# First factor of a 3008-point transform: 32x32 instead of 64x64 TensorE tiles for batches 2 to 7

## The chip, the core and the metric

The kernel runs on one core of a Trainium2 chip. The metric is the device time of one execution in microseconds (us); the median of the runs counts. The engines are called as in the profile: PE is TensorE (matmuls; PEld is its weight load), DVE is VectorE, ACT is ScalarE, POOL is GpSimd and SP is SyncE, which here issues almost all DMAs.

## The reference

Two layers, one behind the other, all in fp32. The first mixes along the sequence with a filter in the frequency domain, the second is a feed-forward layer with ELU.

```python
def _attn_ref(x, filt_r, filt_i):            # x: 8 x 3008 x 256
    X = np.fft.rfft(x, axis=1)
    Y = X * (filt_r + 1j * filt_i)[None, :, :]
    return np.fft.irfft(Y, n=x.shape[1], axis=1).astype(np.float32)

def _moe_ref(x, w_in, w_out):                # x: 24064 x 256, w_in: 256 x 2048
    h = x @ w_in
    g = np.where(h > 0.0, h, np.exp(np.minimum(h, 0.0)) - 1.0)
    return g @ w_out
```

## The kernel before

The 3008 points are taken as 47 x 64. The forward transform has two factors: a 64-point one for each of the 47 residues n1 (the "first factor", with its twiddles), and a 47-point one (the "second factor"); the filter product and the two factors of the inverse follow, and then the feed-forward layer. The residues n1 = i and n1 = 47 - i are worked on together, so 24 pairs i stand for the 47 residues. They are loaded in 6 chunks of 4 pairs (`XC` = 4, `NXC` = 6).

The feed-forward layer is the bulk of the work. It runs in 192 steps, which the code calls quads: 8 batches of 6 blocks, each block with 4 quarters of the 2048 hidden columns. A step has 7 products "up" (`up_steps`, lines 568 to 648, written to the tiles phs, pha and phd by line 583) and the 7 products "down" of the step before it (`down_steps`, lines 653 to 689, written to po by line 665); 7 are enough for a 2x2 blocked product of 8. Each product is two matmul instructions of 128x128 weights and 256 columns (224 in a batch's first block), and each fp32 matmul instruction stands in the trace as two records. ACT and DVE do the ELU and the sums of the seven products.

The transform of batch b is woven into the feed-forward steps of batch b - 1. Nothing is scheduled at run time: the order of every engine is the order of the Python calls. The loop at the end of the kernel goes through the steps and emits the up and down products alternately; the table `plan` says which other pieces go where in a step: place 2 and 3 among the first products, place 0 in the middle, place 1 at the end, behind the DVE and ACT work that the step itself leaves (`up_tail`, `down_tail`). A step in which `opens` holds starts with a down product, to give the banks time. Let t be the first step of batch b - 1. For batches 2 to 7, what matters here is planned so:

- `x_load` (line 202) fetches a chunk of x and its table `ta` of cosines and sines.
- `x_unit` (line 220; DVE lines 223 and 224) forms for a chunk the sum and the difference of points n2 and n2 + 32 (tiles sd and xc). Place 0 of steps t, t + 3 and t + 4, for two chunks each.
- `a_unit` (line 230) is the first factor of two chunks: place 1 of the same steps, so three times a batch. They are called its first, second and third unit below; there are 21 in all, 18 of them for batches 2 to 7.
- `z_write` (line 305; DMA line 311), behind it at place 1, stores the result of the two chunks to DRAM (z); `z_read` (line 313; DMA line 317) brings it back, rearranged, for the second factor. The reads of the first two groups are issued at step t + 4, behind the third unit's writes; then come loads of x for the next batch.
- `b_unit` (line 378) is the second factor, from step t + 6 on, in tiles of 24x32 (sixteen tiles at once, line 388); `bi_unit` (line 450) is the corresponding one of the inverse, also in sixteen tiles (line 460). Both are planned four times a batch.
- `n_unit` (line 522; matmuls in line 535, 64x64 tiles) is the last factor of the inverse. It comes at place 0 of steps t + 1, t + 5, t + 8 and others; it takes two PSUM banks.

One `a_unit` has 16 matmul instructions of 64x64 tiles and 256 columns. A tile's 64 rows hold the points of i (32 rows) and of 47 - i (32 rows), and the 64 columns of its table hold cosines and sines with both signs, so that one matmul does the 64-point factor and joins i with 47 - i at once. Four tiles of the array work side by side. Four ACT copies (line 241) then move the four PSUM banks to two tiles t1 in SBUF.

Four PSUM banks (the list `banks`) serve all pieces but po. `bank()` takes the one that stands first in the list, and each piece appends its banks in the order in which they will be free. In a step, phs holds one bank from the first up product to the sixth, pha one for the second, and phd one from the fifth up product to the last; what a piece at place 1 takes was held by these. [...]

The batches differ at the start: batch 0 has a path of its own (`a_first`), and in the steps in which batch 1 is transformed, DVE and ACT still prepare feed-forward weights (`w_split`, `w_float`, `w_join`, `w_sums`).

Of the kernel before, what the change touches and what calls it, by code (L numbers as in the profile page):

```python
# [11 lines left out]
FP32 = mybir.dt.float32  # L12
U32 = mybir.dt.uint32
AXT = mybir.ActivationFunctionType
# [12 lines left out]
P = 128  # L27
# [14 lines left out]
def _make_tables():  # L42

    n2, k2 = np.arange(N2), np.arange(K2)
    ta, tn = np.zeros((P, H, P)), np.zeros((P, H, P))
    for i in range(H):
        for h in range(2):
            if h and i == 0:
                continue  # L60
            n1 = N1 - i if h else i
            th = 2 * np.pi * (((N1 * n2[:, None] + n1) * k2[None]) % N) / N
            c, s = np.cos(th), -np.sin(th)
            c[:, 0], s[:, 0] = 1.0, 1.0 - 2.0 * (n2 % 2)
            sign = -1.0 if h else 1.0
            r = slice(h * 64, h * 64 + 64)
            for p, v in enumerate((c, sign * s, s, sign * c)):
                ta[r, i, p * 32:p * 32 + 32] = v
                tn[p * 32:p * 32 + 32, i, r] = v.T
    tf = np.ascontiguousarray(ta.reshape(P, H, 4, K2).transpose(0, 1, 3, 2)).reshape(P, H, P)  # L70
    tb = ta.reshape(2, 2, 32, NXC, 2, 2, 4, 16, 2)[:, 0].transpose(3, 0, 1, 2, 4, 7, 5, 6)
    ta = np.ascontiguousarray(tb).reshape(P, H // 2, P)
    i = np.arange(H)[:, None]
    gb, gr, gi = (np.zeros((P, 2, 64)) for _ in range(3))
    q = np.arange(N1)[None]
    th = 2 * np.pi * ((i * np.where(q < 24, q, 70 - q)) % N1) / N1
    c, s = np.cos(th), np.sin(th)
    sign = np.where(q < 24, 1.0, -1.0)
    gb[0:24, 0, :N1], gb[24:48, 0, :N1] = c, s
    gb[64:88, 0, :N1], gb[88:112, 0, :N1] = c * sign, -s * sign  # L80
    for o in (0, 64):
        gr[o:o + N1, 0, 0:24], gr[o:o + N1, 0, 24:48] = 2 / N * c.T, 2 / N * s.T
        gi[o:o + N1, 0, 0:24], gi[o:o + N1, 0, 24:48] = 2 / N * (c * sign).T, -2 / N * (s * sign).T
    k1 = np.arange(24)[None]
    t0 = 2 * np.pi * ((i * k1) % N1) / N1
    t3 = 2 * np.pi * ((i * (32 + 64 * k1)) % N) / N
    c0, s0, c3, s3 = np.cos(t0), np.sin(t0), np.cos(t3), np.sin(t3)
    gb[0:24, 1, 0:24], gb[24:48, 1, 24:48] = c0, c3
    gb[64:88, 1, 24:48], gb[88:112, 1, 0:24] = -s3, -s0

    m0, m3 = np.full((24, 1), 2 / N), np.full((24, 1), 2 / N)
    m0[0] = m3[23] = 1 / N
    s0[:, 0] = s3[:, 23] = 0.0
    gr[0:24, 1, 0:24], gr[24:48, 1, 24:48] = m0 * c0.T, m3 * c3.T
    gi[0:24, 1, 24:48], gi[24:48, 1, 0:24] = -m0 * s0.T, -m3 * s3.T

    fb, bb = np.zeros((P, 2, 32)), np.zeros((P, 2, 4, 32))
    for p in range(4):  # L100
        r = slice(32 * p, 32 * p + 24)
        fb[r, 0, :24] = (-1.0 if p == 3 else 1.0) * gb[24 * (p % 2):24 * (p % 2) + 24, 0, 0:24]
        q = (0, 24, 64, 88)[p]
        k = 24 if p in (1, 2) else 0
        fb[r, 1, :24] = gb[q:q + 24, 1, k:k + 24]
    for o in range(0, P, 32):
        for p, (t, c) in enumerate(((gr, 0), (gr, 24), (gi, 0), (gi, 24))):
            bb[o:o + 24, 0, p, :24] = t[0:24, 0, c:c + 24]

    bb[0:24, 1, 0, :24], bb[0:24, 1, 1, :24] = gr[0:24, 1, 0:24], gr[24:48, 1, 24:48]  # L110
    bb[0:24, 1, 2, :24], bb[0:24, 1, 3, :24] = gi[24:48, 1, 0:24], gi[0:24, 1, 24:48]
    pairs = np.concatenate([fb.reshape(P, 64), bb.reshape(P, 2 * P)], 1)
    lie = np.concatenate([2 * np.arange(24), 2 * np.arange(24) + 1])
    gb[:, :, lie] = gb[:, :, :48].copy()
    for t in (gr, gi):
        for o in (0, 64):
            t[o + lie] = t[o:o + 48].copy()
    gf = np.zeros_like(gb)
    for o in (0, 64):
        gf[o:o + 48] = gb[o:o + 48].reshape(2, H, 2, 64).swapaxes(0, 1).reshape(48, 2, 64)  # L120
    tw = np.ascontiguousarray(tn[:, 0:8].reshape(4, K2, 8, 2, 2, 32).transpose(1, 0, 2, 4, 3, 5)).reshape(P, 8, P)
    tn = tn.reshape(4, K2 // 2, 2, H, 2, 2, 32)[..., 0, :] * np.array([1.0, -2.0])[:, None, None, None]
    tn = np.ascontiguousarray(tn.transpose(2, 1, 0, 3, 4, 5)).reshape(P, H, 64)
    once = np.stack([np.eye(P), gf.reshape(P, P)], 1)
    return [t.astype(np.float32) for t in (ta, tn, np.stack([gb, gr, gi], 1), tf, once, pairs, tw)]


def order(m):
# [5 lines left out]
def kernel(  # L134
# [8 lines left out]
):  # L143
    nc = tc.nc

    ta_d, tn_d, gs_d, tf_d, once_d, pairs_d, tw_d = [
        nc.inline_tensor(t, name=n + "_t").ap()
        for t, n in zip(_make_tables(), ("ta", "tn", "gs", "tf", "once", "pairs", "tw"))
    ]

    def pool(name, bufs, **kw):
# [44 lines left out]
    def bank(name, shape=(P, 2, D)):  # L196
        i = banks.pop(0)
        return i, psM.tile(list(shape), FP32, tag="m%d" % i, name=name)

    def x_load(b, c, queue=nc.sync, place=None):

        t, w = place or (xp.tile([P, 2, 2, D], FP32, tag="xc", name="xc"), tap.tile([P, 2, P], FP32, tag="ta", name="ta"))
        xs[b, c], tas[b, c] = t, w
        queue.dma_start(w, ta_d[:, 2 * c:2 * c + 2, :])
        for h in range(2):
            i = XC * c + 2 * h
            r = slice(64 * h, 64 * h + 32)
            nc.sync.dma_start(t[r].rearrange("p k u d -> p k (u d)"),  # L210
                              raw(x, b * N + i, [[N1 * D, 32], [32 * N1 * D, 2], [1, 2 * D]]))
            r = slice(64 * h + 32, 64 * h + 64)
            for u in range(2):
                if i + u == 0:
                    nc.gpsimd.memset(t[r, :, 0, :], 0.0)
                else:
                    nc.sync.dma_start(t[r, :, u, :],
                                      raw(x, b * N + N1 - i - u, [[N1 * D, 32], [32 * N1 * D, 2], [1, D]]))
# [8 lines left out]

    def a_unit(b, c):  # L230
        ps = [[bank("psa") for _ in range(2)] for _ in range(2)]
        for j in range(2):
            xt, w, sm = xs.pop((b, c + j)), tas.pop((b, c + j)), sds.pop((b, c + j))
            for u in range(2):
                for o, src in ((0, sm), (64, xt[:, 1])):
                    for (_, p), r in zip(ps[j], HALVES):
                        nc.tensor.matmul(p[o:o + 64, u, :], w[r, u, o:o + 64], src[r, u, :], start=True, stop=True)  # L237
        for j in range(2):
            t = t1s[b, c + j] = t1p.tile([P, XC, D], FP32, tag="t1", name="t1")
            for h, (i, p) in enumerate(ps[j]):  # L240
                nc.scalar.activation(out=t[:, 2 * h:2 * h + 2, :], in_=p, func=AXT.Copy)
                banks.append(i)
# [61 lines left out]

    def z_write(b, c):
        if c == 0:
            zs[b] = zp.tile([H, 4 * K2 + 1, D], FP32, tag="z", name="z")
        t = t1s.pop((b, c))
        z = zs[b][XC * c:XC * c + XC, 0:4 * K2, :].rearrange("i (q r) d -> r q i d", r=2)
        for r in range(2):  # L310
            nc.sync.dma_start(z[r], t[HALVES[r]])

    def z_read(b, g):
        t = t2[:, g % 2]
        for p in range(4):
            k = p * K2 + 4 * g
            nc.sync.dma_start(t[32 * p:32 * p + 24].rearrange("i u d -> i (u d)"),
                              zs[b][:, k:k + 4, :].rearrange("i u d -> i (u d)"))

    def f_read_first(g, t):  # L320
        for a, r in enumerate((LO, HI)):
# [517 lines left out]
    with tc.manual_schedule():  # L839
# [153 lines left out]
        for b in range(B):  # L993
            t = (b - 1) * PER
            if b > 0:
                for c, s in enumerate((2, 2, 3, 3, 4, 4) if b == 1 else (0, 0, 3, 3, 4, 4)):
                    at(t + s, 0, x_unit, b, c)
                    if c % 2 == 0:
                        opens.add(t + s + 1)
                        at(t + s, 1, a_unit, b, c)  # L1000
                    if c % 2:
                        for k in (c - 1, c):
                            at(t + s, 1, z_write, b, k)
                        if c == NXC - 1:
                            for k in range(2):
                                at(t + s, 1, z_read, b, k)
                        for k in (c - 1, c):
                            nb, nxt = (b, k + XBUFS) if k + XBUFS < NXC else (b + 1, k + XBUFS - NXC)
                            if nb < B:
                                at(t + s, 1, x_load, nb, nxt)  # L1010
# [91 lines left out]
```

## Time and profile before

| | |
|---|---|
| median of 3 runs | 2559.9 us (2559.11 to 2561.76) |
| the profiled execution's own time | 2560.57 us |
| its span, first to last instruction | 2558.6 us |
| mean granted TensorE clock | 0.997 |
| busy, share of the span | PE 99%, PEld 85%, DVE 81%, ACT 60%, POOL 6% |
| moved by DMA | 200.62 MB, mean 78 GB/s |

Times in rows of the profile are microseconds from the span's start, or a duration in microseconds or nanoseconds as each view says. "L237" is line 237 of the kernel before. "xN" is a count of records, and a matmul instruction has two. The chain of waits follows the work that ended last back from the end of the execution, at each step to what released it; its rows give a start, a length, and the work. A group that waited shows its idle time and who ended it in brackets.

### The profile page before, as it was taken

What the parts mean: (1) busy time and instruction counts of PE and PEld (TensorE: products, weight loads), DVE (VectorE), ACT (ScalarE), POOL (GpSimd) and SP (SyncE); (2) the same over time, 40 slices, a digit from 0 to 9 for tenths busy, and PEclk for the clock granted to TensorE, in tenths of its full rate; (3) what the DMA queues carried; (4) which work ended last, traced back from release to release, by engine and by line L of the source; (5) the groups of instructions that cost most, each with busy time, mean ns of one, the idle gap of its engine ahead of it and who ended that gap; (6) DMA issues with size and microseconds to landing.
All of it is one profiled execution on the core that took longest, in us unless ns stands there. A gap on an engine that the chain in (4) does not pass through costs nothing.

```text
span 2558.6 us, 43997 instructions
## 1 busy us (share of the span) xinstructions
PE 2522.3 (99%) x16690; PEld 2164.8 (85%) x16690; DVE 2066.1 (81%) x3577; ACT 1544.9 (60%) x2716; POOL 160.2 (6%) x315
## 2 busy tenths in 40 slices
PE   6999999999999999999999999999999999999999
PEld 4788889888898888988889888888888888898888
DVE  6978887788878888788887888778897788876766
ACT  7765556655566565665566656565656655555555
POOL 5001000010000000000000000000100011000000
PEclk9999999999999999999999999999999999999999
DMA  9672213522133231433215231343213322110010
GB/s 281 178 189 65 62 39 81 130 67 69 44 102 100 67 69 40 121 82 72 57 44 150 64 80 36 77 122 81 60 41 85 84 63 69 36 46 18 19 28 17
DMA packets 228295, 200.62 MB, mean 78 GB/s; under 512 B 127174, under 2 KB 200406, under 8 KB 228084
## 3 DMA queue, kind: packets, MB, share of 16 engines
q1 hardware_dynamic: 213588, 166.93, 26.6%
q0 software_dynamic: 14000, 30.44, 4.3%
q8 instruction: 131, 2.15, 0.4%
q14 instruction: 80, 0.66, 0.1%
q10 hardware_dynamic: 496, 0.46, 0.1%
HBM read 125.86 MB, written 78.12 MB: 80 GB/s over the span
## 4 chain that ended last, share of the span: by engine, by line
PE 96%; DMA 2%; DVE 1%; ACT 0%; issue 0%; SPq 0%; DVEq 0%; ACTq 0%
PE po L665 45%; PE phs L583 25%; PE phd L583 13%; PE pha L583 6%; PE psn L535 2%; PE psa L237 2%; PE pf L388 1%; PE pv L460 1%; DMA xc<-in_x_dram 1%; DMA x<-in_x_dram 0%; PE po L333 0%; PE po L299 0%; DMA yd<-t 0%; PE psr L333 0%; DMA t<-yd 0%
## 5 line engine op out<-in xcount | busy, mean ns | idle before, releaser
L665 PE MATMUL po<-g,wo 128*128 128x256 f32 (+1 forms) x5376 | 1317.6, 377 | 0.0
L665 PEld LDWEIGHTS po<-g,wo 128*128 128x128 f32 x5376 | 1010.7, 190 | 165.8 <-issue 49.6
L594 ACT ACTIVATE g<-phs 128x512 f32<-128x512 f32 (+1 forms) x576 | 338.8, 588 | 737.1 <-PE phs L583 735.7
L601 ACT ACTIVATE e<-e 128x512 f32<-128x512 f32 (+1 forms) x768 | 477.2, 621 | 24.4
L605 DVE SCALAR_TENSOR_TENSOR g<-e,g 128x512 f32<-128x512 f32 (+1 forms) x576 | 387.3, 672 | 13.8 <-ACT e L601 13.4
L591 DVE TENSOR_TENSOR g<-phd,g 128x512 f32<-128x512 f32 (+1 forms) x384 | 258.7, 674 | 165.1 <-ACT e L601 107.7
L583 PE MATMUL phs<-y,wi 128*128 128x256 f32 (+1 forms) x1536 | 388.4, 375 | 0.0
L583 PE MATMUL phd<-y,wi 128*128 128x256 f32 (+1 forms) x1504 | 380.3, 375 | 0.0
L600 ACT ACTIVATE e<-g 128x512 f32<-128x512 f32 (+1 forms) x576 | 354.4, 615 | 34.1 <-DVE g L591 26.7
L583 PEld LDWEIGHTS phs<-y,wi 128*128 128x128 f32 x1536 | 291.9, 190 | 33.4 <-ACT g L594 0.2
L583 PEld LDWEIGHTS phd<-y,wi 128*128 128x128 f32 x1504 | 284.8, 190 | 35.1 <-DVE g L591 2.6
L605 DVE SCALAR_TENSOR_TENSOR g<-e,phs 128x512 f32<-128x512 f32 (+1 forms) x192 | 129.9, 677 | 115.5 <-ACT e L601 115.5
L583 PE MATMUL phs<-yt,wi 128*128 128x256 f32 (+1 forms) x768 | 193.8, 375 | 0.9 <-ACT g L594 0.9
L583 PE MATMUL phs<-yb,wi 128*128 128x256 f32 (+1 forms) x768 | 193.8, 375 | 0.6 <-ACT g L594 0.6
L583 PE MATMUL pha<-yb,wi 128*128 128x256 f32 (+1 forms) x736 | 185.9, 375 | 0.0
L600 ACT ACTIVATE e<-phs 128x512 f32<-128x512 f32 (+1 forms) x192 | 112.3, 585 | 111.9 <-PE phs L583 111.8
L591 DVE TENSOR_TENSOR g<-pha,g 128x512 f32<-128x512 f32 (+1 forms) x192 | 129.3, 673 | 45.5 <-PE pha L583 45.5
L583 PEld LDWEIGHTS phs<-yt,wi 128*128 128x128 f32 x768 | 145.7, 190 | 17.8 <-ACT g L594 1.2
L583 PEld LDWEIGHTS phs<-yb,wi 128*128 128x128 f32 x768 | 143.9, 190 | 19.3 <-ACT g L594 1.0
L327 POOL DMA_DIRECT2D fall<-fp x224 | 110.5, 501 | 721.9 <-DVE r L433 696.7
L583 PEld LDWEIGHTS pha<-yb,wi 128*128 128x128 f32 x736 | 139.8, 190 | 16.1
L642 DVE TENSOR_TENSOR g<-g,g 128x512 f32<-128x512 f32 (+1 forms) x192 | 130.7, 681 | 6.7
(170 smaller groups left out, 2066.3 us busy)
## 6 DMA issues: line engine op xcount, KB each, us to landing
yd<-t SPq DMA_DIRECT2D x127, 192.0 KB
t<-yd SPq DMA_DIRECT2D x92, 256.0 KB
z<-t SPq DMA_DIRECT2D x84, 256.0 KB
fall<-fp POOLq DMA_DIRECT2D x224, 96.0 KB, 3.0
t<-z SPq DMA_DIRECT2D x224, 96.0 KB
out_dram<-o SPq DMA_DIRECT2D x624, 32.0 KB
xc<-in_x_dram SPq DMA_DIRECT2D x84, 128.0 KB
xc<-in_x_dram SPq DMA_DIRECT2D x161, 64.0 KB
```

Of the source, the lines that this page charges most:

```text
L237: nc.tensor.matmul(p[o:o + 64, u, :], w[r, u, o:o + 64], src[r, u, :], start=True, stop=True)
L327: nc.gpsimd.dma_start(t[32 * a:32 * a + 24].rearrange("p c u d -> p (c u d)"), fp[g, a].rearrange("q c u d -> q (c u d)"))
L388: nc.tensor.matmul(pf[p][1][32 * a:32 * a + 32, js, :], fb[r, v, :], t2[r, js, a, :], start=True, stop=True, tile_position=(32 * p, 32 * a))
L535: nc.tensor.matmul(o, t[r, i - 4 * m, ds(dh * P + 64 * c, 64)], w[r, i - 4 * m, :], start=True, stop=True)
L583: nc.tensor.matmul(ps[:, a, 0:h], w_in[q][:, COMBO[n], a, :], y[n], start=start and a == 0, stop=True, skip_group_check=True)
L591: nc.vector.tensor_tensor(out=g[o], in0=i0, in1=i1, op=ALU.add)
L594: nc.scalar.activation(out=g[o], in_=i0, func=AXT.Copy)
L600: nc.scalar.activation(out=e, in_=src, func=AXT.Relu, scale=-1.0)
L601: nc.scalar.activation(out=e, in_=e, func=AXT.Exp, scale=-1.0)
L605: nc.vector.scalar_tensor_tensor(out=g[n], in0=es[n], scalar=1.0, in1=src, op0=ALU.subtract, op1=ALU.max)
L642: nc.vector.tensor_tensor(out=b12, in0=b22, in1=b12, op=ALU.subtract)
L665: nc.tensor.matmul(po[i][:, u, 0:h], w_out[q][:, COMBO[n], a, :], g[n][:, a, :], start=q == 0 and a == 0 and n in (1, 3, 6, 4), stop=True, ...
```

## The change

For batches 2 to 7 the first factor no longer joins i and 47 - i in the matmul. A tile has 32 rows, one of the two residues, and 32 columns, the cosines and sines of that residue without the signs; the table is half as wide (`tc`, made from `ta` by leaving out every second part). `a_apart` issues 32 matmul instructions of 256 columns in sixteen 32x32 tiles, with row group k always writing bank k: for each half u first the row groups 0 to 2, which use the first three banks, then row group 3, which uses the last. Then, for each of two result tiles, ACT copies the bank of 47 - i to SBUF, and DVE forms the sum and the difference with the bank of i, which it reads from PSUM: two ACT copies and four DVE instructions in all. The banks are handed back in the order 1, 3, 0, 2: the two that ACT alone reads first.

The result has another order: each t1 tile now holds two pairs i of both chunks (64 partitions to each chunk), with sum and difference side by side. `z_write` is called once for the two chunks instead of twice and issues 8 DMAs of 32 partitions instead of 4 of 64; the tile z gets one more row, so that sum and difference are each one block of equal length, and `z_read` picks its four parts from these blocks. Batch 1 keeps the old path, and so do all other pieces.

```diff
+    tc = np.ascontiguousarray(tb[..., 0::2, :]).reshape(P, H // 2, 64)
...
+    def apart(b):
+
+        return b > 1
+
     def x_load(b, c, queue=nc.sync, place=None):
 
         t, w = place or (xp.tile([P, 2, 2, D], FP32, tag="xc", name="xc"), tap.tile([P, 2, P], FP32, tag="ta", name="ta"))
+        if apart(b):
+            w = w.rearrange("p a (s t) -> p (a s) t", s=2)[:, 0:2]
         xs[b, c], tas[b, c] = t, w
-        queue.dma_start(w, ta_d[:, 2 * c:2 * c + 2, :])
+        queue.dma_start(w, (tc_d if apart(b) else ta_d)[:, 2 * c:2 * c + 2, :])
...
+    def a_apart(b, c):
+        ps = [bank("psa") for _ in range(4)]
+        src = [(tas.pop((b, c + j)), (sds.pop((b, c + j)), xs.pop((b, c + j))[:, 1])) for j in range(2)]
+        for u in range(2):
+            for rows in ((0, 1, 2), (3,)):
+                for j, (w, parts) in enumerate(src):
+                    for o in range(2):
+                        for k in rows:
+                            r, a = slice(32 * k, 32 * k + 32), 64 * j + 32 * o
+                            nc.tensor.matmul(ps[k][1][a:a + 32, u, :], w[r, u, 32 * o:32 * o + 32], parts[o][r, u, :],
+                                             start=True, stop=True, tile_position=(32 * k, a))
+        for h in range(2):
+            t = t1s[b, c, h] = t1p.tile([P, XC, D], FP32, tag="t1", name="t1").rearrange("p (u s) d -> p u s d", s=2)
+            one, two = ps[2 * h][1], ps[2 * h + 1][1]
+            nc.scalar.activation(out=t[:, :, 1], in_=two, func=AXT.Copy)
+            nc.vector.tensor_tensor(out=t[:, :, 0], in0=t[:, :, 1], in1=one, op=ALU.add)
+            nc.vector.tensor_tensor(out=t[:, :, 1], in0=one, in1=t[:, :, 1], op=ALU.subtract)
+        banks.extend(ps[k][0] for k in (1, 3, 0, 2))
+
     def a_unit(b, c):
+        if apart(b):
+            return a_apart(b, c)
...
-            zs[b] = zp.tile([H, 4 * K2 + 1, D], FP32, tag="z", name="z")
+            zs[b] = zp.tile([H, 4 * K2 + 2, D], FP32, tag="z", name="z")
+            if apart(b):
+                zs[b] = zs[b].rearrange("i (s k) d -> i s k d", s=2)
+        if apart(b):
+            for h in range(2):
+                t = t1s.pop((b, c, h)).rearrange("p u s d -> p (u s) d")
+                for j in range(2):
+                    i = XC * (c + j) + 2 * h
+                    z = zs[b][i:i + 2, :, 0:2 * K2, :].rearrange("i s (q r) d -> r q (i s) d", r=2)
+                    for r in range(2):
+                        a = 64 * j + 32 * r
+                        nc.sync.dma_start(z[r], t[a:a + 32])
+            return
...
-        for p in range(4):
-            k = p * K2 + 4 * g
-            nc.sync.dma_start(t[32 * p:32 * p + 24].rearrange("i u d -> i (u d)"),
-                              zs[b][:, k:k + 4, :].rearrange("i u d -> i (u d)"))
+        for p, (n, k) in enumerate(((0, 0), (1, K2), (0, K2), (1, 0))):
+            z = zs[b][:, n, k + 4 * g:k + 4 * g + 4] if apart(b) else zs[b][:, p * K2 + 4 * g:p * K2 + 4 * g + 4]
+            nc.sync.dma_start(t[32 * p:32 * p + 24].rearrange("i u d -> i (u d)"), z.rearrange("i u d -> i (u d)"))
...
-                        for k in (c - 1, c):
+                        for k in (c - 1,) if apart(b) else (c - 1, c):
                             at(t + s, 1, z_write, b, k)
```

More of the change, by code (lines that the diff above doesn't have):

```diff
@@ L124, in _make_tables @@
     once = np.stack([np.eye(P), gf.reshape(P, P)], 1)
-    return [t.astype(np.float32) for t in (ta, tn, np.stack([gb, gr, gi], 1), tf, once, pairs, tw)]
+    return [t.astype(np.float32) for t in (ta, tc, tn, np.stack([gb, gr, gi], 1), tf, once, pairs, tw)]
 def order(m):
@@ L144 @@
     nc = tc.nc
-    ta_d, tn_d, gs_d, tf_d, once_d, pairs_d, tw_d = [
+    ta_d, tc_d, tn_d, gs_d, tf_d, once_d, pairs_d, tw_d = [
         nc.inline_tensor(t, name=n + "_t").ap()
-        for t, n in zip(_make_tables(), ("ta", "tn", "gs", "tf", "once", "pairs", "tw"))
+        for t, n in zip(_make_tables(), ("ta", "tc", "tn", "gs", "tf", "once", "pairs", "tw"))
     ]
```

## The prediction

> **What bounds the kernel now.** I read the page's busy times first, then the busy times in the stretch from the first dense step to the end of the last.
>
> ```profile
> PE 2522.3 (99%) x16690; PEld 2164.8 (85%) x16690; DVE 2066.1 (81%) x3577; ACT 1544.9 (60%) x2716; POOL 160.2 (6%) x315
> 134.00:2552.00 2418.00, 2418.00 (x16052) 2083.37 (x16051) 1959.08 (x3370) 1447.66 (x2543) 126.55 (x251) 1.00 0.29 70
> ```
>
> In the second row PE's records cover all 2418.00 us of 2418 (the first figure after the stretch's length), at full clock (1.00): from 134 us on PE never stands still. DVE, third, is busy for 1959 us, 81%. Busy records could still hide matmuls that wait, so I took the chain of waits, its shares by line, and its pieces in order of time around the second and third changed unit of batch 2.
>
> ```profile
> PE po L665 45%; PE phs L583 25%; PE phd L583 13%; PE pha L583 6%; PE psn L535 2%; PE psa L237 2%; PE pf L388 1%; PE pv L460 1%; DMA xc<-in_x_dram 1%; DMA x<-in_x_dram 0%; PE po L333 0%; PE po L299 0%; DMA yd<-t 0%; PE psr L333 0%; DMA t<-yd 0%
> 445.06 1.89 PE psa L237 x32
> ...
> 458.48 1.89 PE psa L237 x32
> 460.37 1.06 PE po L665 x4
> ...
> 467.47 1.09 PE psn L535 x64
> ```
>
> The chain is PE, piece upon piece without a wait. So 1 us less of matmul is 1 us less of time, as long as no other engine then ends last; and 1 us more on DVE costs nothing while it fits into DVE's idle fifth at the right places. A unit of the first factor takes 1.89 us of this chain; 18 of the 21 are changed, 34 us in all.
>
> **The matmuls.** Removed: 18 times 1.89 us. Added: 18 units of 32 instructions (64 records) in sixteen tiles. The trace has no such unit, but both its parts. The old unit shows how records of 256 columns follow each other in one tile, and the inverse's factor in line 460 what sixteen tiles at once cost.
>
> ```profile
> 458.41 0.43 PE L237 MATMUL psa<-sd,ta 64*64 64x256 f32 x2
> ...
> 458.68 0.38 PE L237 MATMUL psa<-sd,ta 64*64 64x256 f32 x2
> ...
> 458.89 0.38 PE L237 MATMUL psa<-sd,ta 64*64 64x256 f32 x2
> ...
> 459.11 0.38 PE L237 MATMUL psa<-sd,ta 64*64 64x256 f32 x2
> ...
> 577.85 1.07 PE pv L460 x32
> ...
> 577.78 1.14 PE L460 MATMUL pv<-zs,pairs 24*32 24x512 f32 x32
> ...
> L460 PE MATMUL pv<-zs,pairs 24*32 24x512 f32 x840 | 31.7, 600 | 0.0
> ```
>
> In the old unit a tile's records start 0, 0.27, 0.48 and 0.70 us after the first (458.41 to 459.11), and one lasts 0.38. Sixteen tiles (line 460) take 1.14 us for two records of 512 columns to a tile; with 0.60 for the last record, 0.54 lies between the first start and the last, 0.43 of it one record's streaming (two times 0.215), so the tiles' starts spread over 0.11. The new unit has four records of 256 columns to a tile: 0.70 + 0.11 + 0.38 = 1.19 from its first start. The chain counts 0.07 less than that (577.78 and 577.85), so **1.12 us a unit, 0.77 saved**.
>
> **A bank that comes late.** The new unit needs its fourth bank at once (row group 3, after 24 records), the old one only for its second half, 0.85 us in. This bank is freed by DVE's last sum of the step, line 591.
>
> ```profile
> 408.42 0.62 DVE L591 TENSOR_TENSOR g<-phd,g 128x448 f32<-128x448 f32 x1
> ...
> 443.79 0.62 DVE L591 TENSOR_TENSOR g<-phd,g 128x448 f32<-128x448 f32 x1
> ...
> 458.04 0.68 DVE L591 TENSOR_TENSOR g<-phd,g 128x512 f32<-128x512 f32 x1
> ...
> 409.90 1.89 PE psa L237 x32
> ...
> 486.03 1.63 PE pf L388 x18
> 487.66 1.06 PE po L665 x4
> ```
>
> In third units the sum ends at 458.72, 0.31 after the unit's first matmul; row group 3 would start at 0.08 and now starts at about 0.36. Its four records then end 0.28 later: 1.40 us, 0.49 saved. In first and second units the block has 224 columns, and the same sum ends at 409.04 and 444.41, 0.8 and 0.6 us ahead of the unit (409.90 and 445.06, less 0.07): no wait. **Sum: 12 x 0.77 + 6 x 0.49 = 12.2 us.** Bounds for a unit: 1.07, as if four records were as cheap as two of twice the length (18 x 0.82 = 14.8 us saved), and 1.63, the longest sixteen-tile unit of the trace (486.03, with special columns and a bank that comes late; 18 x 0.26 = 4.7 us saved). I take the sum, as it is built from the same record lengths. Leaving a unit costs the same either way: the four po records behind it take 1.06 after the old unit (460.37) and after sixteen tiles (487.66).
>
> **DVE and ACT.** ACT loses two of four copies, 2 x 0.6 us a unit. DVE gains four instructions of 128x512, two operands, one in PSUM. The trace has these: r<-r,pf.
>
> ```profile
> L407 DVE TENSOR_TENSOR r<-r,pf 128x512 f32<-128x512 f32 x56 | 38.5, 687 | 1.9
> ...
> L406 DVE TENSOR_TENSOR r<-r,pf 128x512 f32<-128x512 f32 x56 | 38.1, 680 | 0.0
> ...
> 418.04 1.09 PE psn L535 x64
> ...
> 412.76 0.75 DVE L681 TENSOR_TENSOR c<-po,k 128x256 f32<-128x256 f32 x2
> 414.37 0.62 DVE L591 TENSOR_TENSOR g<-pha,g 128x448 f32<-128x448 f32 x1 [0.86 <-PE pha L583]
> ...
> 420.30 0.69 DVE L560 SCALAR_TENSOR_TENSOR yb<-y,y 128x512 f32<-128x512 f32 x1 [4.52 <-ACT y L542]
> ...
> 447.25 0.62 DVE L645 TENSOR_TENSOR g<-g,g 128x448 f32<-128x448 f32 x1
> 449.73 0.69 DVE L591 TENSOR_TENSOR g<-pha,g 128x512 f32<-128x512 f32 x1 [1.86 <-PE pha L583]
> ...
> 455.35 0.69 DVE L591 TENSOR_TENSOR g<-phd,g 128x512 f32<-128x512 f32 x1 [2.27 <-PE phd L583]
> ...
> 462.80 0.68 DVE L681 TENSOR_TENSOR c<-po,k 128x224 f32<-128x224 f32 x2
> ...
> 469.73 0.69 DVE L560 SCALAR_TENSOR_TENSOR yb<-y,y 128x512 f32<-128x512 f32 x1 [4.93 <-ACT y L542]
> ```
>
> Four cost 2.73 us a unit, 49 us in all; DVE rises from 81% to about 83%. They stand behind the step's tail and ahead of the next step's first sum (line 591 on pha), which they delay, and the sums of the block's end (line 681) behind it. They cost nothing because DVE idles there: 0.86 + 4.52 us after first units, 1.86 + 2.27 after second, 4.93 after third, each more than 2.73. Uncovered, they would cost up to 2.73 a unit.
>
> The nearest PE work that waits for them is psn, which takes the last two banks they free: the new code hands on 1 and 3 (freed by ACT alone) to phs and pha, and 0 and 2 (freed by DVE) come next. After a third unit DVE starts the four at 463.48 (462.80 + 0.68) and ends at 466.2; psn, at 467.47 before, would come at 466.98: 0.8 us to spare. After a first unit: 413.51 + 2.73 = 416.2 against 418.04 - 0.77 = 417.3, 1.0 us to spare. After second units no psn follows.
>
> ```profile
> 459.95 2.04 ACT L241 ACTIVATE t<-psa 128x512 f32<-128x512 f32 x4
> ```
>
> ACT's first copy ends at 459.95 + 0.6 = 460.55 as before (ACT is held by the step's tail until then), and phs wants its bank about 1.06 us after the unit's end at 459.88, at 460.9: no wait either.
>
> **DMA.** A unit's stores become eight issues instead of four; table loads halve (36 times 64 KB less). SP's queue around a third unit, the only one that the transform waits for soon:
>
> ```profile
> 461.05 3.67 SPq L311 DMA_DIRECT2D z<-t  x4
> 467.78 3.17 SPq L317 DMA_DIRECT2D t<-z  x8
> ...
> 476.96 0.83 SPq L217 DMA_DIRECT2D xc<-in_x_dram  x2
> 480.75 11.12 SPq L715 DMA_DIRECT2D out_dram<-o  x24
> ```
>
> The first store now waits for two DVE sums, until 464.8 instead of 461.05; eight issues at the old 0.92 each end at 472.2, and the reads, which came 3.1 after the last store's issue, run from 475.3 to 478.5. Their user is pf at 486.03 (row above): 7.5 us of cover less the landing, for 6 units; without it each microsecond late costs one. The loads and stores queued behind move some 7 us back; the loads are for the next batch. I cost all this at nothing.
>
> **Sum against the profiled execution**: 2560.6 - 12.2 = 2548.4. It stood 0.7 above the median of the runs, 2559.9, so the forecast is **2547.7 us**.
>
> **Rivals.** *One: records cannot follow that fast, and nothing is gained.* The row with 64 records is psn, 64 records of 64 columns in 1.09 + 0.07 us:
>
> ```profile
> L535 PE MATMUL psn<-tn,t 64*64 64x64 f32 x2944 | 53.4, 221 | 0.0
> ```
>
> With 0.22 for the last, 63 steps take 0.94 us, 15 ns each; sixteen tiles in line 460 take 0.54 / 31 = 17 ns with a record's streaming in it. Nothing is saved if 64 records take the old unit's 1.96 us: with 0.38 for the last, 1.58 / 63 = 25 ns a step; the time is then 2559.9. The two rows speak against it. [...]
>
> *Two: the two halves u do not overlap*, because the second half's weights wait behind row group 3. Each half then costs 0.27 + 0.11 + 0.38 = 0.76 by itself, 1.52 less 0.07 is 1.45 a unit: 12 x 0.44 + 6 x 0.16 = 6.2 saved, 2553.7. For it: weights and matmuls are issued in one order. Against: in the old unit's rows a tile's third record follows the second at the streaming rate, its weights loaded in between.
>
> *Three, the slower side: DVE's sums hold the banks that psn wants.* The place is psn after first and third units, 12 in all, and the margin is 1.0 and 0.8 us. If an instruction took 1.3 us (readers of PSUM delayed by matmuls, say), four would take 5.2, psn would wait 5.2 - 2.73 - 0.9 = 1.6 us, 12 times: 19 us, net 7 slower, **2566.5**. It decides from 1.16 us an instruction (12.2 / 12 = 1.0 beyond the margin). Against: no DVE row of 128x512 above takes more than 0.69, with PSUM or without.
>
> **Chances.** Forecast 0.77, rival one 0.07, two 0.08, three 0.08. A measurement of this kernel tells about 0.2% from no change, 5 us. Faster: the forecast but for 0.03 and most of rival two, 0.81; the same: rival one and these, 0.10; slower: 0.09. The range goes from the low bound (2545.1) with half a microsecond to the high one (2555.2): 2544.5 to 2555.5, which holds rival two as well.
>
> **What would show it.** In the new chain, the psa piece of batches 2 to 7 has 64 records and 1.1 us in first and second units, 1.4 in third; 1.9 would be rival one, 1.45 everywhere rival two. DVE's busy time rises by 49 us to about 2115, ACT's falls by some 21 to 1523; PE has no gap ahead of psn, and the pieces behind a unit keep their lengths. I am wrong if PE shows idle time before psn or phs, if pf waits for t<-z, or if the four sums take more than 0.7 us.

## The result, and the profile after

| | before | changed |
|---|---|---|
| median of 7 runs each | 2560.34 us | 2551.56 us |
| lowest and highest | 2558.62, 2568.51 | 2549.42, 2553.43 |
| profiled execution's own time | 2560.57 | 2553.3 |
| its span | 2558.6 | 2551.5 |

The ratio is 0.9963 (95% interval 0.9951 to 0.9974): faster by 0.37%, 8.8 us between the medians and 7.3 between the two profiled executions. The forecast was 2547.7, a gain of 12.2, with a range of 2544.5 to 2555.5.

Lines have moved: the new matmuls are in line 246, the new copies and sums in lines 251 to 253; batch 1's matmuls are in line 265. Up products now stand in line 622, down products in 704, psn in 574. The page's busy times first, then the stretch from the first dense step to the end of the last:

```profile
PE 2517.5 (99%) x17266; PEld 2162.0 (85%) x17266; DVE 2112.0 (83%) x3649; ACT 1527.3 (60%) x2680; POOL 159.4 (6%) x315
```

```profile
134.00:2545.00 2411.00, 2411.00 (x16628) 2078.38 (x16628) 2005.24 (x3442) 1430.07 (x2507) 125.91 (x251) 1.00 0.28 69
```

PE still covers all of its stretch at full clock (2411.00 of 2411), DVE has 46 us more and ACT 18 less. So the kernel is bound as before, and the gain must be read from the chain of waits, in order of time (start, length, work), around the three units of batch 2:

```profile
410.10 1.42 PE psa L246 x61
411.52 0.95 PE po L704 x4
...
444.79 1.43 PE psa L246 x60
...
457.75 1.59 PE psa L246 x60
459.34 1.06 PE po L704 x4
...
466.44 1.09 PE psn L574 x64
```

(The trace has all 64 records of each unit; the chain counts 60 or 61, those that lengthen it.) A unit took 1.89 us before; now it takes 1.42, 1.43 and 1.59. That is 6 x (0.47 + 0.46 + 0.30) = 7.4 us, all of the 7.3 between the profiled executions: nothing was lost anywhere else. What is behind a unit keeps its length (0.95 and 1.06). So the whole miss lies inside the units: 1.12 us had been expected in first and second units and 1.40 in third.

Every record's start inside the first unit, in us from its first record, shows where:

```
changed, first unit of batch 2, 64 records
records  1 to 16  0.00 0.01 0.01 0.02 0.03 0.03 0.04 0.05 0.05 0.06 0.07 0.07 0.08 0.09 0.09 0.10
records 17 to 32  0.24 0.25 0.25 0.26 0.27 0.27 0.28 0.29 0.29 0.30 0.31 0.31 0.32 0.33 0.33 0.34
record  33        0.46
records 34 to 64  0.65 0.67 0.67 0.68 0.70 ... 1.09 1.10 1.12
end               1.49
```

The first half (records 1 to 32, two for each of sixteen tiles) runs as predicted. Then only the first tile's third record starts at the streaming rate, 0.22 after its second. The next starts at 0.65, and from there tiles follow every 17 ns instead of every 7. (A unit runs 0.07 us longer by its records than by the chain.)

### The profile page after: what moved, and what is told of

The parts are those of the page before. It is cut to its first block, busy times and chain, and to the rows that moved or that the text cites. A ratio compares the mean times of both kernels' runs of the same rounds, so it can differ in the third digit from the quotient of the medians.

```text
span 2551.5 us, 45225 instructions
## 1 busy us (share of the span) xinstructions
PE 2517.5 (99%) x17266; PEld 2162.0 (85%) x17266; DVE 2112.0 (83%) x3649; ACT 1527.3 (60%) x2680; POOL 159.4 (6%) x315
## 4 chain that ended last, share of the span: by engine, by line
PE 97%; DMA 2%; DVE 1%; SPq 0%; issue 0%; ACT 0%; DVEq 0%
PE po L704 45%; PE phs L622 25%; PE phd L622 13%; PE pha L622 6%; PE psn L574 2%; PE pf L427 1%; PE pv L499 1%; DMA xc<-in_x_dram 1%; PE psa L246 1%; PE po L372 1%; DMA x<-in_x_dram 1%; PE po L327 0%; PE psr L372 0%; PE psa L265 0%; PE psa L308 0%
```

## The experiments

The question was what holds the second half back. Times below are medians, each with the kernel before on the same chip; "unit" is the piece of the chain, for first, second and third unit of batch 2.

| run | its time | before | ratio, 95% interval | unit |
|---|---|---|---|---|
| changed kernel | 2551.56 | 2560.34 | 0.9963 [0.9951, 0.9974] | 1.42, 1.43, 1.59 |
| u innermost | 2565.72 | 2559.08 | 1.0025 [1.0016, 1.0035] | 2.25, 2.25, 2.25 |
| row groups in pairs | 2556.69 | 2559.08 | 0.9990 [0.9981, 1.0000] | 1.72, 1.72, 1.75 |
| one table, 512 columns | 2547.53 | 2559.08 | 0.9952 [0.9937, 0.9967] | 1.07, 1.07, 1.54 |
| a third round | 2563.42 | 2559.08 | 1.0014 [1.0005, 1.0024] | 2.06, 2.06, 2.22 |
| row groups together | 2553.16 | 2560.06 | 0.9971 [0.9959, 0.9982] | 1.42, 1.42, 1.74 |
| sums doubled | 2580.05 | 2560.06 | 1.0081 [1.0066, 1.0096] | |
| sums alone, from PSUM | 2599.90 | 2560.06 | 1.0154 [1.0139, 1.0169] | 1.89 (old tiles) |
| sums alone, in SBUF | 2559.00 | 2559.61 | 0.9995 [0.9986, 1.0004] | 1.89 (old tiles) |
| banks swapped | 2632.43 | 2559.61 | 1.0277 [1.0256, 1.0297] | |
| batch 1 too | 2555.61 | 2560.06 | 0.9986 [0.9976, 0.9995] | 1.42, 1.42, 1.59 |

**Both halves of a tile together.**

```diff
-        for u in range(2):
-            for rows in ((0, 1, 2), (3,)):
-                for j, (w, parts) in enumerate(src):
-                    for o in range(2):
-                        for k in rows:
+        for rows in ((0, 1, 2), (3,)):
+            for j, (w, parts) in enumerate(src):
+                for o in range(2):
+                    for k in rows:
+                        for u in range(2):
```

> The unit's 32 matmuls in another order: both halves u of a tile one directly behind the other, tile by tile; nothing left out. In the changed kernel a unit takes 1.43 us of PE's chain (1.59 in third units), 0.31 more than predicted, and the late part is the second half: the first tile's third record starts on time, 0.46 us after the unit's first, those of the other fifteen only from 0.65 on. Theory A, places: PE holds at most 64 instructions (16 matmuls of two weight loads and two records each) that are not finished, and frees their places in order, so the 18th matmul waits for the end of the second record of the first matmul. Then eight tiles fill all places here, the other eight start only when the first tile's fourth record has ended, about 1.05 us in, and a unit takes about 2.2 us: time 2551.6 + 18 x 0.75 = 2565. Theory B, a boundary (rival two of the prediction): the second half of the banks has to wait for the first half, or behind row group 3. Then here, without such a boundary, a unit takes about 1.12 (1.4 in third units) and the time is about 2547. Theory C, supply: after the first instructions, which lie ready, matmuls come no faster than 17 ns apart. Then a unit takes about 1.2 and the time is about 2548.

Its chain of waits:

```profile
408.48 2.25 PE psa L246 x64
```

The unit takes 2.25 us, longer than with 64x64 tiles, and the time is 2565.7: theory A's numbers (2.2 and 2565), and 17 us and more from those of B and C. Record starts in this unit, put to tiles by their spacing, duration and operands:

```
u innermost, first unit of batch 2
first tile       0.00 0.24 0.46 0.67    (the last ends at 1.05)
tiles 2 to 8     0.01 to 0.09 (first record), 0.25 to 0.33, 0.47 to 0.55, 0.69 to 0.77
ninth tile       0.42 0.64 0.86 1.07    (matmuls 17 and 18)
tiles 10 to 16   1.08 1.11 1.15 1.18 1.21 1.25 1.28 (first record)
```

The tenth tile has nothing ahead of it, yet it starts only at 1.08, just after the first tile's fourth record (0.67 + 0.37 = 1.05) has ended. Between tiles PE did not keep to the order of its instructions: here the second matmul, in the first tile, started at 0.46, behind the first records of seven later ones (0.01 to 0.09).

**Row groups in pairs.**

```diff
-        for u in range(2):
-            for rows in ((0, 1, 2), (3,)):
+        for rows in ((0, 1), (2, 3)):
+            for u in range(2):
```

> Order of the unit's matmuls: row groups 0 and 1 with both halves u, then row groups 2 and 3 with both halves; nothing left out. Theory A (64 places): the first 16 matmuls now hold both halves of eight tiles, so the third records of all eight start on time, about 0.46 us after their first, and it is the first records of the other eight tiles that come late, at about 0.65 us and after; a unit takes about 1.7 us, time about 2556. Theory B (boundary between the halves): the third records of the eight tiles are late, as in the changed kernel. Theory C (supply): a unit takes about 1.2 us, time about 2548.

```profile
410.28 1.72 PE psa L246 x60
```

Now eight tiles get both halves among the first 16 matmuls. Record starts in this unit:

```
row groups in pairs, first unit of batch 2
records  1 to 16  0.00 ... 0.05 (eight tiles, first record)   0.24 ... 0.29 (second)
record  17        0.42 (ninth tile, first record)
records 18 to 25  0.46 0.46 0.47 0.48 0.48 0.49 0.50 0.50 (eight tiles, third record)
```

The third records come on time for all eight, with the change of u in between, so no boundary between the halves exists. The seventeenth matmul now belongs to a new tile, and it starts at 0.42; the rest of the new tiles follow from 0.65. The same place in the order of instructions is late, whatever it works on. Theory B is out, and C as the whole cause too (1.72 instead of 1.2).

**Half the instructions.**

```diff
-        for u in range(2):
...
-                            nc.tensor.matmul(ps[k][1][a:a + 32, u, :], w[r, u, 32 * o:32 * o + 32], parts[o][r, u, :],
+                        nc.tensor.matmul(ps[k][1][a:a + 32], w[r, 0, 32 * o:32 * o + 32], parts[o][r],
```

> 16 matmuls of 512 columns in place of 32 of 256: the second pair of every two is multiplied by the first pair's table, so its own twiddles are left out. The same columns stream through the same sixteen tiles, with half the instructions (64 records and loads). All theories: a unit takes 1.07 to 1.12 us in first and second units as in the inverse's factor (1.07), and about 1.35 in third units, where row group 3 waits for its bank; time 2551.6 - 12 x 0.33 - 6 x 0.24 = 2546. It gives what the second 16 matmuls cost beyond their streaming. If the unit stays at 1.4, the cost is not one of the number of instructions, and all three theories are wrong.

```profile
406.68 1.07 PE psa L245 x32
...
453.76 1.54 PE psa L245 x30
```

The same columns through the same tiles in 16 instructions take 1.07 us, so the second 16 cost 0.35 beyond their streaming in first and second units. Third units come out at 1.54 instead of 1.35: I had not worked out what a bank 0.3 us late does to a unit of 512-column records, and this part of the expectation missed. The time (2547.5; expected 2546) is the forecast's.

**A third round.**

```diff
-        for u in range(2):
+        for u in (0, 1, 1):
```

> The second half's 16 matmuls are issued a second time over the same place, with the same result; nothing left out. Theory A (64 places): each further 16 matmuls wait for places, so a round costs not its streaming of 0.43 us but the time from a matmul's first start to the end of its second record, about 0.64: a unit takes 2.07 us, time 2551.6 + 18 x 0.64 = 2563. Theory B (each half on its own): 0.76 a round, a unit of 2.2, time 2565. Theory C (supply): a round costs its streaming, a unit of 1.86, time 2559.5.

```profile
410.84 2.06 PE psa L246 x88
```

A further 16 matmuls cost 0.64 us (2.06 - 1.42) where their streaming is 0.43: A's number (2.07), not C's (1.86) or B's (2.2). It is the time from a matmul's first record to the end of its second, 0.24 + 0.37 = 0.61, and the 0.03 until the next starts.

Together the four show theory A at work: **in these units sixteen matmuls were under way at once, and behind them a place came free only when the oldest had ended**. The 64 instructions are an estimate from these starts. The traces show a weight load and a record, twice, for each of these matmuls (64 PEld and 64 PE records for the 32 matmuls of the changed kernel's unit), so 16 matmuls are 64 instructions. The starts speak for instructions being counted, and not whole matmuls. The seventeenth matmul's first record is the 66th instruction; where its tile is free (the runs with u innermost and in pairs) it starts at 0.42, just behind the end of the second instruction, the first matmul's first record (0.40). In the changed kernel and in pairs the eighteenth matmul and all behind it start from 0.65 on, when the first matmul's second record has ended (0.61). The profile models the ends of matmuls; the two starts lie 0.02 and 0.04 us behind them.

Theory A alone is not the whole miss. Behind the first sixteen, matmuls follow each other at 17 ns in these runs (tiles at 33 ns with u innermost, where each has two), though in the changed kernel the first sixteen matmuls' second records start, and by theory A places come free, every 7 ns (0.24 to 0.34 us). This is the rate that theory C spoke of. In the changed kernel the wait for the first free place is 0.19 us (the eighteenth matmul starts at 0.65 instead of 0.46), and the slower succession of the fourteen tiles behind it makes 14 x 0.010 = 0.14. What sets the 17 ns no run here shows.

**Row group 3 among the others.**

```diff
-            for rows in ((0, 1, 2), (3,)):
+            for rows in ((0, 1, 2, 3),):
```

> Row group 3 is issued among the others in each half instead of behind them; nothing left out. Theory A (64 places): first and second units stay at 1.43 us; in third units the whole first half waits for row group 3's bank, 0.3 us after the fourth matmul, so 1.7 instead of 1.59: time within 1 us of 2551.6. Rival two as the prediction put it (the second half's weights wait behind row group 3): first and second units fall to about 1.12, time about 2548.

```profile
409.80 1.42 PE psa L246 x60
444.49 1.42 PE psa L246 x60
457.45 1.74 PE psa L246 x61
```

First and second units stay at 1.42, so the second half does not wait behind row group 3. Third units rise to 1.74 as A has it (1.7); the time, 2553.2, is 1.6 above 2551.6, where 1 had been allowed. The order in the changed kernel is worth 0.15 us a third unit.

**What the sums cost.** The prediction put DVE's sums at nothing. Four runs ask why that held, and how near the other side was.

```diff
+            for _ in range(3):
-            nc.vector.tensor_tensor(out=t[:, :, 0], in0=t[:, :, 1], in1=one, op=ALU.add)
+                nc.vector.tensor_tensor(out=t[:, :, 0], in0=t[:, :, 1], in1=one, op=ALU.add)
```

> The two sums of a unit are each formed three times, so DVE has eight instructions a unit instead of four, 2.73 us more; nothing left out. This asks how far the changed kernel is from rival three, DVE's sums holding the banks that psn wants. In the changed kernel's profile the four end 1.05 us ahead of psn after a third unit (465.39 against 466.44) and 1.43 us after a first (416.34 against 417.77). If those margins are all the cover there is, psn waits 2.73 - 1.05 = 1.7 us six times and 1.3 us six times: time 2551.6 + 18 = 2570, and up to 8 us more if second units lose their cover too. If DVE's idle time as a whole is the cover, the time stays at 2551.6.

PE's waits, in all, times, and the longest:

```profile
PE psn L575 <- DVE t L254: 17.5, 12, 1.7
...
PE phd L623 <- DVE g L631: 7.8, 8, 1.7
```

psn waits for the sums twelve times, 17.5 us in all, which is the 18 expected from the margins. The phd waits grow by 5.5 (2.3 before, 7.8 now): that is the cover of second units going. The time is 2580, 28 more than the changed kernel, where 18 to 26 had been expected. The waits are 23 of it. PE's clock falls to half after one of them, in batch 2, which makes that batch 1.7 us longer than the others (264.14 instead of 262.45 from the third unit to the next; see the last section). The rest, 0.1 to 0.3 us behind each wait, is not explained.

The kernel before with the sums alone, first on the PSUM banks, then on the SBUF copies:

```diff
                 nc.scalar.activation(out=t[:, 2 * h:2 * h + 2, :], in_=p, func=AXT.Copy)
+                if b > 1:
+                    nc.vector.tensor_tensor(out=t[:, 2 * h:2 * h + 2, :], in0=t[:, 2 * h:2 * h + 2, :], in1=p, op=ALU.max)
                 banks.append(i)
```

> The kernel before, with 64x64 tiles and four ACT copies, and four DVE instructions more in each unit of batches 2 to 7 that read the same banks (a maximum of each copy with its own source, which changes nothing) and free them: the change's DVE work without its matmuls, stores and loads. By the prediction the four are covered by DVE's idle time: as the kernel before, within 0.1%. If DVE's sums take back part of the gain, this is slower than before by that part (up to 2.73 x 18 = 49 us, were nothing covered).

```profile
PE phs L585 <- DVE t L243: 28.5, 18, 2.7
```

This missed by 40 us. PE's waits name the place: 18 times, once a unit, phs waits for DVE's instruction on the first bank. In the old order the first bank handed back goes to phs at once, and DVE comes to it only after the step's tail. The waits are 28.5 of the 40 us; half clock behind four of them (0.50 from 466 to 469 us in batch 2) adds 1.7 each (265.6 instead of 263.9 from a third unit to the next), and the remaining 5 are not explained. That made two theories, and two runs.

```diff
+                    z = t[:, 2 * h:2 * h + 2, :]
+                    nc.vector.tensor_tensor(out=z, in0=z, in1=z, op=ALU.max)
```

> The kernel before with four DVE instructions more in each unit of batches 2 to 7, as in the run before that came out 40 us slower, but now on the copies in SBUF (a maximum of each with itself, which changes nothing), so that ACT alone frees the banks, as it did. Theory D, banks: those 40 us came from phs, the next step's first product, which takes the first bank handed back, and that bank was DVE's to free, behind the step's tail; 2.73 us of DVE work by itself is covered. Then this run is as the kernel before, within 0.1%. Theory E, capacity: DVE has no room for four more instructions a unit in the kernel before. Then this run is slower by the same 40 us or nearly.

2559.0 against 2559.6: four more DVE instructions a unit cost nothing measurable here, where ACT alone frees the banks.

```diff
-        banks.extend(ps[k][0] for k in (1, 3, 0, 2))
+        banks.extend(ps[k][0] for k in (0, 2, 1, 3))
```

> The changed kernel with its banks handed back in the order 0, 2, 1, 3 instead of 1, 3, 0, 2; nothing left out. Theory D (banks): phs and pha now take the two banks that DVE's sums free. In the changed kernel's profile phs starts at 412.47, 447.16 and 460.40 after the three units, and DVE ends the first two sums at about 415.0, 448.9 and 464.1: phs waits 2.5, 1.7 and 3.7 us, after the longest wait some 2 us more at half clock as in the run with the sums alone: 10 us a batch, time 2551.6 + 60 = 2610. Theory E (capacity): the order changes nothing, 2551.6.

```profile
PE phs L622 <- DVE t L253: 50.6, 18, 3.8
...
PE pha L622 <- DVE t L253: 2.8, 10, 0.3
```

In this kernel only the order of four numbers differs from the changed one, and it is 73 us slower than the kernel before. phs waits 50.6 us, the waits per unit being 2.70, 1.91 and 3.82 in batch 2 where 2.5, 1.7 and 3.7 were expected. The total is 81 instead of 60 over the changed kernel. From each of the three units to the next, batches 3 to 6 take 3.5, 2.6 and 6.5 us longer than there, where 2.5, 1.7 and 5.7 had been worked out; and in batches 2 and 7 half clock follows the two shorter waits too, for 1.7 and 1.2 more (in batch 2 four records behind them take up to 1.49 and 1.71 us instead of 0.76 and 0.86). So the sums are free by the order in which banks are handed back, not by DVE's idle time alone.

**Batch 1 too.**

```diff
-        return b > 1
+        return b > 0
```

> The new tiles for batch 1 too; nothing left out. By the matmuls alone three more units save 0.46, 0.46 and 0.3 us: 2550.3. But in these steps DVE has no idle time in the kernel before: from 119 to 140 us it never waits, after the first of the three units. So the four sums of the first unit, 2.73 us, and those of the second push everything behind them, and psn or the next unit waits: up to 5 us, time up to 2555. If it comes out at 2550, DVE's cover is not what limits the change to batches 2 to 7.

PE's waits in this kernel, and in the changed one:

```profile
PE phd L622 <- DVE g L630: 5.4, 2, 3.7
```

```profile
PE phd L622 <- DVE g L630: 2.3, 2, 1.7
```

Three more units save 0.47 + 0.46 + 0.30 = 1.2 us of matmul, but phd, and not psn as expected, now waits 3.1 us more, for DVE, after the first of them. Its time of 2555.6 is 4.0 above the changed kernel's; from separate chips a difference of this size is not sure. The traces show the direction: from batch 1's first unit to batch 2's it takes 289.8 us (119.9 to 409.7), and the changed kernel 287.9 (122.1 to 410.0), 1.9 less, which is 3.1 of waits less 1.2 of matmul. The two spans are equal (2551.5) only because this execution reached its first unit 2.2 us earlier. Faster it is not. No version tried here that computes the reference beats the changed kernel.

## Why the prediction was right, and where a size was off

**The bound.** Right. PE has no gap after the change either, and the chain's difference in psa is the difference in time.

**The matmuls.** Right in kind, too small in size. The step that failed is the sentence "The new unit has four records of 256 columns to a tile: 0.70 + 0.11 + 0.38": the term 0.70, the spacing of four records in one tile, came from the old unit, which has 16 matmuls in all and so none behind a sixteenth. With 32 matmuls the second half waits for places (0.19 us) and then follows at 17 ns a matmul instead of 7 (0.14). Measured, the last record starts at 1.12 instead of 0.81 (1.49 - 0.37, against 0.70 + 0.11), and the unit takes 1.42 instead of 1.12. The range held the result since its upper bound had been taken from another unit (1.63), not since this wait had been foreseen. The low bound, "as if four records were as cheap as two of twice the length", is what the run with 512 columns gives (1.07), and it needs half the instructions.

**The late bank.** The mechanism was right: in third units row group 3 starts at 0.37 us (0.36 predicted). Its price was 0.17 (1.59 against 1.42) instead of 0.28, since the second half is late anyway.

**DVE and ACT.** Right. The four sums take 677 and 692 ns in the mean; in third units they run from 462.66 and end at 465.39, psn starting at 466.44.

```profile
L253 DVE TENSOR_TENSOR t<-psa,t 128x512 f32<-128x512 f32 x36 | 24.9, 692 | 1.2
...
L252 DVE TENSOR_TENSOR t<-t,psa 128x512 f32<-128x512 f32 x36 | 24.4, 677 | 0.0
...
464.70 0.69 DVE L253 TENSOR_TENSOR t<-psa,t 128x512 f32<-128x512 f32 x1
465.30 0.68 DVE L630 TENSOR_TENSOR g<-pha,g 128x512 f32<-128x512 f32 x1
```

The margin came out at 1.05 us where 0.8 had been worked out. But the reason given first, that DVE's idle time covers them, is half of it; the other half, the order of the banks, stood there as a detail of where psn's banks come from, and the last pair of runs shows that it decides 81 us.

**DMA.** Right that it costs nothing, too dear in detail. SP's queue around a third unit:

```profile
464.10 4.45 SPq L346 DMA_DIRECT2D z<-t  x8
470.46 3.15 SPq L357 DMA_DIRECT2D t<-z  x8
```

Eight issues of half the size take 4.45 us (0.56 each, not 0.92), and the reads run at 470.46, 4.8 us earlier than worked out. pf, their user, starts at 485.00.

**The rivals.** Rival one (nothing gained) is out: records start 7 ns apart in the first half. Rival two gave 1.45 a unit and 2553.7, nearly what came, but by another mechanism: the halves do overlap, and nothing waits behind row group 3, as the runs with the order changed show. Rival three did not occur, and its price was well placed: at twice the sums psn waits twelve times, as it said, for 17.5 us. What it left out are second units, after which phd then waits (5.5 us).

## What to carry to other kernels

When a matmul is cut into more and smaller tiles, count the instructions under way, not the columns alone: here 16 fp32 matmuls, 64 instructions by the estimate above, were under way at once, and beyond them a round of sixteen cost the 0.64 us from start to end instead of the 0.43 of its streaming. Work moved from PE to a less busy engine was free here only where that engine did not free the buffer that PE asked for next (the sums alone: 2559.0 us on the SBUF copies, 2599.9 on the PSUM banks; the changed kernel: 2551.6, and 2632.4 with the banks swapped); hand back first what an early, idle engine frees. And a unit's price that is built from units with half the instructions, as here, missed what the second sixteen cost: 1.42 us measured, 1.12 worked out.

## What the runs showed of the hardware that had not been expected

**The order of instructions decided by a factor.** The same 32 matmuls took 1.42, 1.72 or 2.25 us by their order alone: in the slowest order the tenth tile, with nothing ahead of it, stood idle until 1.08, just behind the end of the first tile's fourth record (1.05).

**A wait of PE cost more than itself.** In the run with banks swapped, busy times and granted clock (the figure before the last two) in the stretches behind a wait of 3.8 us:

```profile
473.00:474.00 1.00, 1.00 (x4) 0.81 (x3) 0.00 (x0) 0.42 (x1) 0.00 (x0) 0.50 0.97 268
474.00:475.00 1.00, 1.00 (x4) 0.82 (x3) 0.40 (x1) 0.00 (x0) 0.00 (x0) 0.50 0.97 259
475.00:476.00 1.00, 1.00 (x4) 0.73 (x4) 0.96 (x3) 0.00 (x0) 0.00 (x0) 0.50 0.75 204
476.00:477.00 1.00, 1.00 (x6) 0.90 (x5) 0.01 (x1) 0.00 (x0) 0.00 (x0) 0.99 0.00 0
```

The clock is at 0.50 until about 476, with the first matmuls back at 470.7, and each group of four records takes 1.7 to 2.0 us instead of 0.86:

```profile
470.74 2.04 PE phs L622 x4
472.79 1.71 PE pha L622 x4
474.49 1.68 PE po L704 x4
476.17 0.86 PE phs L622 x4
```

With doubled sums a wait of 1.67 us was enough once, in batch 2, and the low clock came a good microsecond after PE had resumed:

```profile
469.00:470.00 1.00, 0.77 (x51) 0.77 (x55) 1.00 (x3) 0.00 (x0) 0.00 (x0) 1.00 0.56 143
470.00:471.00 1.00, 1.00 (x28) 0.84 (x21) 0.47 (x2) 0.57 (x2) 0.00 (x0) 0.76 0.90 200
471.00:472.00 1.00, 1.00 (x3) 0.74 (x3) 0.45 (x1) 1.00 (x3) 0.00 (x0) 0.50 0.74 191
472.00:473.00 1.00, 1.00 (x4) 0.79 (x3) 0.67 (x2) 0.66 (x2) 0.00 (x0) 0.50 0.57 131
473.00:474.00 1.00, 1.00 (x4) 0.81 (x3) 0.03 (x1) 0.00 (x0) 0.00 (x0) 0.53 0.08 20
```

In the other five batches the same wait leaves the clock at 1.00, and so do the waits of 1.25 us (psn of first units). In this run, the one with banks swapped and the one with the sums alone from PSUM, the clock fell after all six waits of 3.8 us, for 6.8 us each; after six of the twelve waits of 2.7, two of the six of 1.9 and one of the six of 1.67, for 3.4 us each; and after none of the shorter ones. So the length of a wait alone does not decide. In the swapped kernel 53 us of waits on DVE made 81 us of time. The mean granted clock of the profiled execution was 0.987 with banks swapped and 0.994 with the sums alone, against 0.997 in the changed kernel. Stops of 1.67 to 2.70 us within busy work were sometimes enough; what else decides no run here shows.
